# Transposing DMAs for half of x's first chunk, wq on a second queue and q in two passes, in a fused attention and GLU kernel

## The chip, the cores and the metric

The kernel runs on one core of one Trainium2 chip. The metric is device time in microseconds, the median of several executions. One execution is also profiled by the hardware; durations and waits come from that one.

## The reference

x is 2048 tokens of 512 features in bfloat16 (`A_x`; `B_x` is not read). Two branches work on the same x and are mixed by a gate per token:

```python
g = _sigmoid((x * gate_w).sum(-1, keepdims=True))
a = _A_ref(x, A_wq, A_wk, A_wv, A_wo, A_beta)
b = _B_ref(x, B_W_gate, B_W_up, B_W_down)
return g * a + (1 - g) * b
```

Branch A is attention with 32 heads of 16 features over four segments of 512 tokens: q, k and v are products of x with 512x512 weights; inside a segment the heads do causal softmax attention, and across segments a memory M and its normalizer z collect phi(k)·v and phi(k) of the earlier segments, which phi(q) reads. Both results are blended by a gate per head and multiplied by wo. Branch B is a gated linear unit: relu(x W_gate) * (x W_up), 1792 wide, times W_down.

## The kernel before

One program without loops on the chip. Python code lists every operation with its cost, its reads and its writes; a planner (`Sched`, lines 129 to 541) then walks through simulated time and decides, engine by engine, which ready operation comes next. It adds the semaphore waits, and so the order of the instructions on every engine is fixed when the kernel is built. The planner breaks ties by a pseudo-random number from `seeds` (line 567), one seed for each 8 us (`WIN`) of planned TensorE time; beyond the end of the tuple the last seed is used. `LAND0` (line 36) tells the planner how long after issue some of the first loads land, in ns; other loads get general figures. A DMA takes one of 16 semaphores.

Tokens are cut into four chunks of 512 that are also the segments. For each, the work is: the projections `proj` (L793 for q and k, with features on partitions; L791 for v, with tokens on partitions), the attention visits of `att` (L913 scores in row-tiled matmuls, L929 exp on ACT, L935 masks on POOL, L969 P·V, L979 and the following lines on DVE, ending in `oT`), the memory terms (L836, L856), the GLU (`ffn`, L1043 with L1051 to L1054), and `outp`, which sums W_down's product (L1082) and wo's product (L1075) in one PSUM bank, scales it (L1091, L1092) and stores it (L1094). A score visit takes four PSUM banks and is listed ahead of the rest of PE's work; the GLU's and projections' matmuls fill the time between visits.

The head, up to some 13 us, is what the change touches:

- Loads. SP issues two loads of x's first chunk, 256 KB each, tokens on partitions (`hT0` and `hT2`, which borrow the tile hT), then wq, wk, wv in four loads of 128 KB each, the first halves of W_gate and W_up, and more. ACT issues three 1 KB loads (`touch0` to `touch2`) and begins with an activation that loads its table (`tab`).
- `warm`: eleven matmuls on constants (L693) while the loads are on their way.
- Transposes of x's first chunk on TensorE: for each half h of 256 tokens and each kt of four blocks of 128 features two matmuls with an identity (L707) into a bank; DVE or ACT then copies the bank to xT (L714), which has features on partitions. The half h is a range of tokens, `xT0_{kt}` for h = 0 and `xT0_{kt + 4}` for h = 1. The later chunks of x come by transposing DMAs of 128 KB each (L621).
- q of the first segment: 16 matmuls of 512 tokens, kt outermost, the four columns of 128 features innermost. Each waits for wq's block kt and both halves of x's block kt. Then k, column by column, two kt to an operation, waiting for all of xT; then v.

Of the kernel before, what the change touches and what calls it, by code (L numbers as in the profile page):

```python
# [32 lines left out]
H1_T = 14000.0  # L33
LX = 300.0
DCOST = {"ldwg0_0": 1000.0, "ldbraw": 1800.0, "ldgwb": 1300.0, "ldx1_0": 1500.0, "vsh0": 1100.0, "vsh1": 1100.0, "vsh2": 1100.0, "vsh3": 1100.0}
LAND0 = {"ldhT0": 2850.0, "ldhT2": 3100.0, "ldwq0": 3150.0, "ldwq1": 3200.0, "ldwq2": 3100.0, "ldwq3": 3000.0}
NBLK = 36
QTN, EKN, HTN, OTN, XR = 8, 4, 19, 8, 3
SBX = 0
# [521 lines left out]
def build_kernel(nc, A_x, A_wq, A_wk, A_wv, A_wo, A_beta, W_g, W_u, W_d, gate_w, out):  # L561
    _, S, D = A_x.shape
    F = W_g.shape[1]
    assert D == 512 and S % 512 == 0 and F % 128 == 0
    NSEG, KT, NF, NT = S // 512, D // 128, F // 128, S // 128
    EPS, SCALE = 1e-6, 16 ** -0.5
    sc = Sched(seeds=(237719, 74891, 0, 89398, 0, 53401, 416309, 0, 0, 0, 710933, 0, 718714, 120896, 538430, 820480, 585027, 870794, 793690, 0, 589972, 0, 0, 0, 454998, 16783, 0,))
    T = {}
    with contextlib.ExitStack() as stack:
        for name, shape, dt in plan(S, D, F):  # L570
            T[name] = stack.enter_context(nc.sbuf_tensor(name, shape, dt))
        PS = stack.enter_context(nc.psum_tensor("ps", [128, 8, 512], F32))
        for st in sc.streams:
            sc.sem[st] = stack.enter_context(nc.semaphore(f"s_{st}"))
        program(sc, nc, T, PS, A_x, A_wq, A_wk, A_wv, A_wo, A_beta, W_g, W_u, W_d, gate_w, out, NSEG, KT, NF, NT, EPS, SCALE)
        with nc.Block() as block:
            sc.emit(block)
    return sc


def program(sc, nc, T, PS, A_x, A_wq, A_wk, A_wv, A_wo, A_beta, W_g, W_u, W_d, gate_w, out, NSEG, KT, NF, NT, EPS, SCALE):
# [19 lines left out]
    def act(fn, occ, **k):  # L601
        return op("act", fn, occ, **k)
# [15 lines left out]
    def load(eng, names, dst, src, nbytes, occ=474.0):  # L618
        (lact if eng == "act" else lsp).append(dma(eng, lambda e, dst=dst, src=src: e.dma_start(dst, src), nbytes, occ=occ, writes=names, name="ld" + names[0]))
# [5 lines left out]
        for kt in range(KT):  # L625
            load_xt("sp", c, kt)
    x0 = A_x[0, 0:512, :].rearrange("(h p i) d -> h p i d", h=2, i=2)
    for h in range(2):
        load("sp", [f"hT{2 * h}", f"hT{2 * h + 1}"], V.hT[:, 2 * h:2 * h + 2, :], x0[h], 1 << 18)
    for eng, nm, w, src in (("sp", "wq", V.wq, A_wq), ("sp", "wk", V.wk, A_wk), ("sp", "wv", V.wv, A_wv)):  # L630
        for kt in range(KT):
            load(eng, [f"{nm}{kt}"], w[:, kt, :], src[kt * 128:(kt + 1) * 128, :], 1 << 17)
    half = (NF // 2) * 128
# [9 lines left out]
    load("sp", ["gwb"], V.gwb[:, :], gate_w.partition_broadcast(128), 1 << 17)  # L643
    load("sp", ["braw"], V.braw[:], A_beta.partition_broadcast(128), 8192)
    load_gu(1)
    lact.insert(0, act(lambda e: e.activation(V.eb[:, 0:8], nc.const_aps.tensor(1.0, [128, 8], BF16), ACT.Exp), 1450, writes=["eb"], name="tab"))
    for n, w in enumerate((W_g, W_u, W_d)):
        load("act", [f"touch{n}"], V.adT[0:16, 32 * n:32 * n + 32], w[0:16, 0:32], 1024)
    sc.queue(0, lact)
    sc.queue(0, lsp)  # L650
    lsp = []
# [43 lines left out]
        return pe(fn, m * n * (0.834 if k == 0 else 0.5), writes=[f"bankL{b}"], name=f"warm{k}")  # L695

    xps, xcs = [warm(5, 512, 0, 3), warm(6, 128, 0, 3)], {"dve": [], "act": []}
    for h, kt, bank, eng in ((0, 0, 0, "dve"), (0, 1, 1, "act"), (0, 2, 2, "act"), (1, 0, None, "dve"), (0, 3, 3, "dve"), (1, 1, 0, "act"), (1, 2, 1, "dve"), (1, 3, 2, "act")):
        ep = Epoch("att") if bank is None else None
        bk = [] if bank is None else [f"bankL{bank}"]  # L700

        def B(ep=ep, bank=bank):
            return A(ep) if bank is None else PL[:, bank, :]

        def fx(e, h=h, kt=kt, B=B):
            for i in range(2):
                ins = e.matmul(B()[:, 128 * i:128 * i + 128], lhsT=V.hT[:, 2 * h + i, kt * 128:(kt + 1) * 128], rhs=V.ident[:], start=True, stop=True)  # L707
            return ins
        xps.append(pe(fx, 205, reads=[f"hT{2 * h}", "ident"], writes=bk, name=f"xt{4 * h + kt}", ep=ep, role=ep and "w"))
        dst = V.xT[:, kt, h * 256:(h + 1) * 256].rearrange("q (t i) -> q t i", i=2)  # L710

        def cpy(e, d=dst, B=B, eng=eng):
            x = B()[:, 0:256].rearrange("q (i t) -> q t i", i=2)
            return e.tensor_copy(d, x) if eng == "dve" else e.activation(d, x, ACT.Copy)  # L714
        xcs[eng].append(op(eng, cpy, 430 if eng == "dve" else 390, reads=bk, writes=[f"xT0_{kt + 4 * h}"], name=f"xc{4 * h + kt}", ep=ep, role=ep and "r"))
# [63 lines left out]
    def proj(s):  # L779
        pes, evs, sbs, acts, sps = [], [], [], [], []  # L780
        tok = s % XR * 512

        def pj(w, col, name, wname, tokmajor=False):
            early = s == 0 and name == "q"
            ep = Epoch("proj", 1, col) if s == 0 and name == "k" and col < 2 else Epoch("att" if early else "proj")
            step = 1 if early else 2
            for k0 in range(0, KT, step):
                def fn(e, k0=k0):
                    for kt in range(k0, k0 + step):
                        if tokmajor:  # L790
                            ins = e.matmul(A(ep)[:, :], lhsT=V.xT[:, kt, tok + col * 128:tok + (col + 1) * 128], rhs=w[:, kt, :], start=(kt == 0), stop=(kt == KT - 1))  # L791
                        else:
                            ins = e.matmul(A(ep)[:, :], lhsT=w[:, kt, col * 128:(col + 1) * 128], rhs=V.xT[:, kt, tok:tok + 512], start=(kt == 0), stop=(kt == KT - 1))  # L793
                    return ins
                pes.append(pe(fn, mm(512, step), reads=[f"{wname}{kt}" for kt in range(k0, k0 + step)] + ([f"xT0_{k0}", f"xT0_{k0 + 4}"] if early else xt(s)), name=f"{name}{s}_{col}", ep=ep, role="w2" if k0 else "w"))
            return ep
        def cp(fn, **k):
            return sc.add(Op([("dve", lambda e: fn(e, e.tensor_copy), t_dve(512)), ("act", lambda e: fn(e, lambda d, x: e.activation(d, x, ACT.Copy)), t_act(512))], **k))
        for G in range(4):
            ep = pj(V.wq, G, "q", "wq")  # L800
            qs = qslot(s, G)
            evs.append(cp(lambda e, f, ep=ep, qs=qs: f(V.qT[:, qs, :], A(ep)[:, :]), writes=[f"qT{qs}"], name=f"qcp{s}_{G}", ep=ep, role="r"))
            if s > 0 and G % 2:
                phi(s, "q", G, V.phiq, "phiq", V.qT, qs - 1, [f"qT{qs - 1}", f"qT{qs}"], acts, sbs)
            ep = pj(V.wk, G, "k", "wk")
            evs.append(cp(lambda e, f, ep=ep, G=G: f(V.kT[:, G, :], A(ep)[:, :]), writes=[f"kT{G}"], name=f"kcp{s}_{G}", ep=ep, role="r"))
            ks = kslot(s, G)
            kv = V.kT[:, G, :].rearrange("q (c k) -> q c k", c=8)
            for p in range(2):
                km = lambda e, kv=kv, p=p, ks=ks: e.tensor_scalar(V.kp[:, ks, :, 64 * p:64 * p + 64], kv, V.pm[:, p:p + 1], None, ALU.mult)  # L810
                ka = lambda e, kv=kv, p=p, ks=ks: e.activation(V.kp[:, ks, :, 64 * p:64 * p + 64], kv, ACT.Copy, scale=V.pm[:, p:p + 1])
                evs.append(sc.add(Op(([("dve", km, 380), ("act", ka, 715)] if s else [("dve", km, 380)]), reads=[f"kT{G}", "pm"], writes=[f"kp{ks}_{p}"], name=f"kmask{s}_{G}_{p}")))
            if s < NSEG - 1 and G % 2:
                phi(s, "k", G, V.ek, "ek", V.kT, G - 1, [f"kT{G - 1}", f"kT{G}"], acts, sbs)
                for g in (G - 1, G):
                    sps.append(dma("sp", lambda e, g=g: e.dma_start_transpose(V.phik[:, :, g * 128:(g + 1) * 128], V.ek[:, g % EKN, :]), 1 << 17, occ=1400.0, reads=[f"ek{g % EKN}"], writes=[f"phik{g}"], name=f"kT2{s}_{g}"))
        for tt in range(4):
            ep = pj(V.wv, tt, "v", "wv", True)
            evs.append(cp(lambda e, f, ep=ep, tt=tt: f(V.vaug[:, s % 2, tt, :, 0:16], A(ep)[:, :].rearrange("q (h c) -> q h c", c=16)), writes=[f"va{s % 2}_{tt}"], name=f"vcp{s}_{tt}", ep=ep, role="r"))
        if s == 0:  # L820
            qp = [[p for p in pes if p.name == f"q0_{col}"] for col in range(4)]
            pes = [qp[col][kt] for kt in range(4) for col in range(4)] + [p for k in "kv" for p in pes if p.name[0] == k]
        return pes, evs, sbs, acts, sps

    def va(s):
# [377 lines left out]
```

## Time and profile before

| | us |
|---|---|
| median of 3 executions | 264.2 (264.17 to 264.76) |
| the profiled execution | 264.5 |
| its span, first to last instruction | 262.7 |
| PE busy in the span | 255.7 |
| ACT busy | 184.5 |
| DVE busy | 179.1 |
| POOL busy | 131.0 |
| PE's first matmul on data (L707) | 3.69 |
| q's first matmul | 5.43 |
| k's first matmul | 9.48 |
| first score visit | 12.60 |

The span is a little shorter than the time of the execution that it belongs to, since the time holds what lies around the program too. A row of the timeline is: start in us, duration in us, engine, line, operation, tile written and tiles read, shapes, number of instructions merged into the row, and in brackets the idle time ahead of it with what ended it. PE is the matmuls, PEld the loads of the stationary operand, which overlap them; SPq and ACTq are the queues that issue DMAs. DMA traffic is heaviest at the start: the DMA engines' mean busy share is 0.69 in the first 8 us and 0.96 in the next 8.

### The profile page before, as it was taken

To read this page: it belongs to the slowest core of one execution; us is meant where nothing else is said; L and a number is where in the kernel's file an instruction comes from. 1 tells how busy PE (TensorE), PEld (TensorE's weight loads), DVE (VectorE), ACT (ScalarE), POOL (GpSimd) and SP (SyncE) were. 2 spreads that over 40 slices of the span, in tenths; PEclk is the share of its full clock that TensorE was granted. 3 is DMA by queue.
4 is the path that set the end of the run, shared out by engine and by line. 5 is a ranking of instruction groups with operands and counts; after the bars stand their busy time and mean duration, and the time that the engine had idled before them with its cause. 6 is when DMAs were issued, how large, how long until landed. Compare 5 with 4: busy or idle time off the path is not lost.

```text
span 262.7 us, 6432 instructions
## 1 busy us (share of the span) xinstructions
PE 255.7 (97%) x2619; PEld 114.6 (44%) x2653; DVE 179.1 (68%) x356; ACT 184.5 (70%) x160; POOL 131.0 (50%) x295
## 2 busy tenths in 40 slices
PE   8999999999999999999999999999999999999996
PEld 5444443444443544334444544443444444344444
DVE  5488878789986587778788676757667716477600
ACT  4586689999789779785768787677777665676021
POOL 3036557564646466666555457836365354545100
PEclk9999999999999999999999999999999999999999
DMA  6989646930261134213040242010131101000011
GB/s 197 286 302 281 138 66 148 274 44 22 68 155 25 24 81 117 48 22 33 10 107 13 59 91 23 4 40 2 31 76 40 22 24 34 26 2 2 0 42 40
DMA packets 34925, 19.87 MB, mean 76 GB/s; under 512 B 24016, under 2 KB 34128, under 8 KB 34896
## 3 DMA queue, kind: packets, MB, share of 16 engines
q1 hardware_dynamic: 34800, 19.46, 30.4%
q8 instruction: 21, 0.34, 0.6%
q14 instruction: 8, 0.07, 0.1%
q10 hardware_dynamic: 96, 0.00, 0.0%
HBM read 10.40 MB, written 2.11 MB: 48 GB/s over the span
## 4 chain that ended last, share of the span: by engine, by line
PE 97%; issue 1%; DVE 1%
PE ps L1043 38%; PE ps L1082 19%; PE ps L793 11%; PE ps L913 9%; PE ps L969 6%; PE ps L791 5%; PE ps L1075 5%; PE ps L856 1%; PE ps L693 1%; PE ps L707 1%; PE ps L836 0%; DVE hT L1054 0%; DVE Tn L979 0%; DVE osb L746 0%; DVE osb L1091 0%
## 5 line engine op out<-in xcount | busy, mean ns | idle before, releaser
L935 POOL TENSOR_SCALAR_AFFINE_SELECT E<-E 64x256 bf16<-64x256 bf16 (+1 forms) x256 | 111.1, 445 | 111.9 <-ACT E L929 82.7
L929 ACT ACTIVATE E<-ps 128x2048 bf16<-128x2048 f32 x72 | 135.1, 1876 | 38.7 <-PE ps L913 38.6
L1043 PE MATMUL ps<-xT,wu 128*128 128x512 bf16 x213 | 57.2, 380 | 1.4 <-issue 1.3
L1043 PE MATMUL ps<-xT,wg 128*128 128x512 bf16 x219 | 57.7, 380 | 0.6 <-issue 0.3
L1082 PE MATMUL ps<-wd,hT 128*128 128x512 bf16 (+2 forms) x229 | 52.8, 367 | 0.9 <-issue 0.6
L1054 DVE TENSOR_TENSOR hT<-ps,rl 128x512 bf16<-128x512 f32 x56 | 38.5, 687 | 16.5 <-PE ps L1043 16.4
L1082 PEld LDWEIGHTS ps<-wd,hT 128*128 128x128 bf16 x238 | 21.4, 98 | 23.8 <-issue 2.4
L1043 PEld LDWEIGHTS ps<-xT,wg 128*128 128x128 bf16 x224 | 20.6, 98 | 25.7 <-issue 2.8
L1043 PEld LDWEIGHTS ps<-xT,wu 128*128 128x128 bf16 x224 | 20.1, 98 | 25.4 <-issue 3.5
L913 PE MATMUL ps<-qT,kp 32*128 32x192 bf16 (+7 forms) x512 | 28.6, 287 | 0.0
L979 DVE STREAM_TRANSPOSE Tn<-ps 128x512 f32<-128x512 f32 x32 | 21.3, 696 | 9.1 <-PE ps L969 9.1
L1052 DVE TENSOR_SCALAR rl<-ps 128x512 bf16<-128x512 f32 x30 | 20.7, 690 | 8.2 <-PE ps L1043 7.9
L1091 DVE TENSOR_SCALAR osb<-ps,omg 128x512 bf16<-128x512 f32 (+1 forms) x8 | 5.6, 700 | 26.0 <-PE ps L1082 15.1
L1051 ACT ACTIVATE rl<-ps 128x512 bf16<-128x512 f32 x26 | 15.5, 598 | 9.9 <-PE ps L1043 9.7
L913 PEld LDWEIGHTS ps<-qT,kp 32*128 32x128 bf16 x512 | 8.2, 92 | 25.3 <-issue 13.1
L969 PE MATMUL ps<-E,vaug 64*17 64x128 bf16 (+7 forms) x512 | 18.7, 283 | 0.0
L969 PE MATMUL ps<-E,vsh 64*17 64x128 bf16 (+7 forms) x512 | 18.3, 283 | 0.0
L1092 ACT ACTIVATE osb<-ps,omg 128x512 bf16<-128x512 f32 (+1 forms) x9 | 6.1, 675 | 16.4 <-PE ps L1075 14.0
L793 PE MATMUL ps<-xT,wq 128*128 128x512 bf16 x61 | 16.1, 391 | 0.4 <-issue 0.3
L1075 PE MATMUL ps<-wo,oT 128*128 128x512 bf16 (+2 forms) x67 | 16.2, 366 | 0.2 <-issue 0.2
L793 PE MATMUL ps<-xT,wk 128*128 128x512 bf16 x60 | 15.6, 380 | 0.4 <-issue 0.3
L791 PE MATMUL ps<-wv,xT 128*128 128x512 bf16 x63 | 15.3, 380 | 0.1
(68 smaller groups left out, 229.2 us busy)
## 6 DMA issues: line engine op xcount, KB each, us to landing
vsh<-vaug SPq DMA_DIRECT2D x8, 272.0 KB, 4.3
osb<-in_A_x_dram SPq DMA_DIRECT2D x16, 128.0 KB, 2.3
out_dram<-osb SPq DMA_DIRECT2D x15, 128.0 KB, 1.7
wg<-in_B_W_gate_dram SPq DMA_DIRECT2D x8, 224.0 KB, 5.0
wu<-in_B_W_up_dram SPq DMA_DIRECT2D x8, 224.0 KB, 5.9
wd<-in_B_W_down_dram SPq DMA_DIRECT2D x1, 1792.0 KB, 10.5
hT<-in_A_x_dram SPq DMA_DIRECT2D x2, 256.0 KB, 3.0
wq<-in_A_wq_dram SPq DMA_DIRECT2D x4, 128.0 KB, 3.3
```

Of the source, the lines that this page charges most:

```text
L791: ins = e.matmul(A(ep)[:, :], lhsT=V.xT[:, kt, tok + col * 128:tok + (col + 1) * 128], rhs=w[:, kt, :], start=(kt == 0), stop=(kt == KT - 1))
L793: ins = e.matmul(A(ep)[:, :], lhsT=w[:, kt, col * 128:(col + 1) * 128], rhs=V.xT[:, kt, tok:tok + 512], start=(kt == 0), stop=(kt == KT - 1))
L913: ins = q.matmul(dst, lhsT=V.kp[r, kslot(s, G), c, :], rhs=V.qT[r, qslot(s, G), q0:q0 + w], start=True, stop=True, tile_position=(32 * jj, ...
L929: acts.append(act(lambda a: a.activation(V.E[:, base * 512:base * 512 + min(2048, 4 * W)], PF[:, 0:min(2048, 4 * W)], ACT.Exp, scale=SCALE ...
L935: pools.append(pool(lambda g, ap=ap, lim=lim, pat=pat: g.affine_select(out=ap, in_=ap, compare_op=ALU.is_ge, fill=0.0, base=lim, pattern=[ ...
L969: ins = q.matmul(A(eps[p])[32 * jj:32 * jj + 17, 64 * (c + u):64 * (c + u + n)], lhsT=v[:, 8 * G + 2 * jj + p, :], rhs=V.E[r, f:f + 64 * n ...
L979: ds.append(dve(lambda e, p=p, ep=eps[p]: e.transpose(V.Tn[:, 2 * (G % (TNN // 2)) + p, :], A(ep)[:, :]), t_dve(512), writes=[f"Tn{2 * (G ...
L1043: ins = e.matmul(A(ep)[:, :], lhsT=w[:, kt, f * 128:(f + 1) * 128], rhs=V.xT[:, kt, c % XR * 512:(c % XR + 1) * 512], start=(kt == 0), sto ...
L1052: ("dve", lambda e, ep=eg, r=r: e.tensor_scalar(V.rl[:, r, :], A(ep)[:, :], 0.0, None, ALU.max), t_dve(512))],
L1054: evs.append(dve(lambda e, ep=eu, r=r, hs=hs: e.tensor_tensor(V.hT[:, hs, :], A(ep)[:, :], V.rl[:, r, :], ALU.mult), t_dve(512), reads=[f" ...
L1075: ins = e.matmul(A(ep)[:, 0:c1 - c0], lhsT=V.oT[:, ot[G], i * 128:(i + 1) * 128], rhs=V.wo[:, G, c0:c1], start=st_ and G == 0, stop=sp_ an ...
L1082: ins = e.matmul(A(ep)[:, 0:c1 - c0], lhsT=V.hT[:, slots[f], i * 128:(i + 1) * 128], rhs=V.wd[:, f, c0:c1], start=st_ and f == f0, stop=sp ...
```

## The change

The second half of x's first chunk (tokens 256 to 511) no longer comes through hT, TensorE and a copy. Four transposing DMAs on SP, one for each block of 128 features, 64 KB each, write it to xT directly; they stand behind `hT0`'s load and ahead of wk's. Four of the eight transposing operations on PE (eight matmuls) and four copies go; the remaining four copies are all DVE's. wq's four loads go to ACT's queue, behind `touch0`, and `tab` goes behind all of ACT's loads. q's products are made in two passes of 256 tokens, first all kt and columns for the first half of the tokens, then for the second, 32 matmuls for 16; each waits for its own half alone. The first two columns of k are issued kt by kt, the two columns side by side. The planner's landing times for the first loads are restated, and its tuple of seeds is a new one of 33 numbers for 27, so the order of instructions after the head is another one too.

```diff
-LAND0 = {"ldhT0": 2850.0, "ldhT2": 3100.0, "ldwq0": 3150.0, "ldwq1": 3200.0, "ldwq2": 3100.0, "ldwq3": 3000.0}
+LAND0 = {"ldhT0": 2950.0, "ldxb0": 3900.0, "ldxb1": 3950.0, "ldxb2": 4000.0, "ldxb3": 4050.0, "ldwq0": 2900.0, "ldwq1": 3150.0, "ldwq2": 3400.0, "ldwq3": 3700.0, "ldwk0": 3900.0, "ldwk1": 3900.0, "ldwk2": 3900.0, "ldwk3": 3950.0}
...
-    for h in range(2):
-        load("sp", [f"hT{2 * h}", f"hT{2 * h + 1}"], V.hT[:, 2 * h:2 * h + 2, :], x0[h], 1 << 18)
-    for eng, nm, w, src in (("sp", "wq", V.wq, A_wq), ("sp", "wk", V.wk, A_wk), ("sp", "wv", V.wv, A_wv)):
+    load("sp", ["hT0", "hT1"], V.hT[:, 0:2, :], x0[0], 1 << 18)
+    for kt in range(KT):
+        lsp.append(dma("sp", lambda e, kt=kt: e.dma_start_transpose(V.xT[:, kt, 256:512], A_x[0, 256:512, kt * 128:(kt + 1) * 128]), 1 << 16, occ=660.0, writes=[f"xT0_{kt + 4}"], name=f"ldxb{kt}"))
+    for eng, nm, w, src in (("act", "wq", V.wq, A_wq), ("sp", "wk", V.wk, A_wk), ("sp", "wv", V.wv, A_wv)):
...
-    lact.insert(0, act(lambda e: e.activation(V.eb[:, 0:8], nc.const_aps.tensor(1.0, [128, 8], BF16), ACT.Exp), 1450, writes=["eb"], name="tab"))
+    tab = (act(lambda e: e.activation(V.eb[:, 0:8], nc.const_aps.tensor(1.0, [128, 8], BF16), ACT.Exp), 1450, writes=["eb"], name="tab"))
     for n, w in enumerate((W_g, W_u, W_d)):
         load("act", [f"touch{n}"], V.adT[0:16, 32 * n:32 * n + 32], w[0:16, 0:32], 1024)
+    lact = lact[4:5] + lact[:4] + lact[5:] + [tab]
...
-    for h, kt, bank, eng in ((0, 0, 0, "dve"), (0, 1, 1, "act"), (0, 2, 2, "act"), (1, 0, None, "dve"), (0, 3, 3, "dve"), (1, 1, 0, "act"), (1, 2, 1, "dve"), (1, 3, 2, "act")):
+    for h, kt, bank, eng in ((0, 0, 0, "dve"), (0, 1, 1, "dve"), (0, 2, 2, "dve"), (0, 3, 3, "dve")):
...
-            step = 1 if early else 2
+            first = s == 0 and name == "k" and col < 2
+            step = 1 if early or first else 2
...
+                if early:
+                    for h in range(2):
+                        def fh(e, k0=k0, h=h):
+                            return e.matmul(A(ep)[:, 256 * h:256 * h + 256], lhsT=w[:, k0, col * 128:(col + 1) * 128], rhs=V.xT[:, k0, 256 * h:256 * h + 256], start=(k0 == 0), stop=(k0 == KT - 1))
+                        pes.append(pe(fh, mm(256), reads=[f"{wname}{k0}", f"xT0_{k0 + 4 * h}"], name=f"{name}{s}_{col}", ep=ep, role="w2" if k0 + h else "w"))
+                    continue
...
-            pes = [qp[col][kt] for kt in range(4) for col in range(4)] + [p for k in "kv" for p in pes if p.name[0] == k]
+            kp = [[p for p in pes if p.name == f"k0_{col}"] for col in range(2)]
+            pes = [qp[col][2 * kt + h] for h in range(2) for kt in range(4) for col in range(4)] + [kp[col][kt] for kt in range(4) for col in range(2)] + [p for k in "kv" for p in pes if p.name[0] == k and p.name not in ("k0_0", "k0_1")]
```

More of the change, by code (lines that the diff above doesn't have):

```diff
@@ L566, in build_kernel @@
     EPS, SCALE = 1e-6, 16 ** -0.5
-    sc = Sched(seeds=(237719, 74891, 0, 89398, 0, 53401, 416309, 0, 0, 0, 710933, 0, 718714, 120896, 538430, 820480, 585027, 870794, 793690, 0, 589972, 0, 0, 0, 454998, 16783, 0,))
+    sc = Sched(seeds=(140892, 423927, 526636, 0, 0, 29334, 773274, 197051, 969207, 716731, 932006, 619180, 627323, 133294, 0, 462444, 160517, 80860, 908900, 0, 153406, 228141, 875880, 487918, 463495, 96319, 0, 0, 0, 804673, 0, 975897, 0,))
     T = {}
@@ L794, in fn @@
                     return ins
-                pes.append(pe(fn, mm(512, step), reads=[f"{wname}{kt}" for kt in range(k0, k0 + step)] + ([f"xT0_{k0}", f"xT0_{k0 + 4}"] if early else xt(s)), name=f"{name}{s}_{col}", ep=ep, role="w2" if k0 else "w"))
+                if early:
[4 more added lines that the diff above has]
+                    continue
+                pes.append(pe(fn, mm(512, step), reads=[f"{wname}{kt}" for kt in range(k0, k0 + step)] + xt(s), name=f"{name}{s}_{col}", ep=ep, role="w2" if k0 else "w"))
             return ep
```

## The prediction

> **What bounds the kernel now.** I read the page's first parts, then the engine waits of PE, then the timeline of the first 14 us.
>
> ```profile
> span 262.7 us, 6432 instructions
> PE 255.7 (97%) x2619; PEld 114.6 (44%) x2653; DVE 179.1 (68%) x356; ACT 184.5 (70%) x160; POOL 131.0 (50%) x295
> ...
> PE 97%; issue 1%; DVE 1%
> ```
>
> PE is busy for 97% and the chain that ended last is PE for 97%. The 7.0 us without PE are 0.84 at the start, 2.2 after the last matmul (260.46, by the timeline of the end) and 4.0 between. The waits of PE tell what the 4.0 are (us in total, times, longest):
>
> ```profile
> PE ps L1043 <- issue: 1.6, 10, 0.2
> PE ps L693 <- PEq L1188: 0.8, 1, 0.8
> ...
> PE ps L1043 <- DVE Tn L979: 0.2, 1, 0.2
> ```
>
> Only one entry, of 0.2 us, is a wait for data of another engine; the rest are gaps of about 0.16 us when PE comes back from a row-tiled visit (the scores of L913, the P·V of L969). So the time follows PE's own work and the number of its visits. The stage that the change touches is the head; its PE and PEld rows (start, us, engine, line, tiles, count):
>
> ```profile
> 0.84 2.93 PE L693 MATMUL ps<-const-bfloat16-1.0 128*128 128x512 bf16 x11 [0.84 <-PEq L1188]
> 3.69 1.95 PE L707 MATMUL ps<-ident,hT 128*128 128x128 bf16 x16
> ...
> 5.43 4.21 PE L793 MATMUL ps<-xT,wq 128*128 128x512 bf16 x16
> ...
> 5.86 0.15 PEld L793 LDWEIGHTS ps<-xT,wq 128*128 128x128 bf16 x1 [0.28 <-issue]
> 6.29 0.15 PEld L793 LDWEIGHTS ps<-xT,wq 128*128 128x128 bf16 x1 [0.28 <-issue]
> 6.68 2.47 PEld L793 LDWEIGHTS ps<-xT,wq 128*128 128x128 bf16 x12 [0.24 <-issue]
> ```
>
> PE runs without a break from 0.84 on. Its weight loads stand 0.43 us apart up to 6.29 and then twelve stand in 2.47 (0.21 each): until about 6.7 us a 512-column matmul takes 0.43, afterwards 0.216. The granted clock reads 1.00 in every stretch, so only this spacing shows the slow start. In the chain of waits the head has no hole either:
>
> ```profile
> 3.77 1.87 PE ps L707 x16
> 5.64 5.30 PE ps L793 x22
> ...
> 256.53 2.28 PE ps L1082 x14
> ...
> 259.46 0.78 PE ps L1082 x14
> ```
>
> A PE transpose costs 1.87 / 16 = 0.117 us there. The last two lines are 14 matmuls of 384 and of 128 columns at the full clock: 0.163 and 0.056 each, new weights for every one.
>
> **The change, part by part.**
>
> *Eight PE transposes go* (h = 1: four tiles, two matmuls each). At 0.117 that is 0.94 us of slow-clock time. If the clock still rises at 6.7, what moves into that time would otherwise run at the double rate: 0.47. Followed through: transposes 3.77 to 4.71; the first copy is ready at 4.12 + 0.42 = 4.54, so q starts at 4.71. In the 2.0 us to 6.7 it does 2.0 / 0.215 = 9.3 half matmuls.
>
> *q in halves.* 32 matmuls of 256 columns for 16 of 512. No row has this form at the full clock; between the 0.056 of 128 columns and the 0.163 of 384 lies 0.109, and half of 0.216 is 0.108: sixteen more instructions cost 0.02 us at that, and (0.163 - 0.109) x 22.7 = 1.2 us if the weight load (98 ns busy in its row) could no longer hide and a half took as long as 384 columns. I take 0.109, as the 128-column row shows weights hidden under a still shorter matmul. The other 22.7 halves take 2.47, and q ends at 9.17. Before: 5.64 + 2.5 x 0.43 + 13.5 x 0.216 = 9.63. **Head: -0.46.**
>
> Rule and row: the Trainium skill, "TensorE: Matmul & The Clock Gate", section "Part 1: The HAM clock gate (the "warmup" mystery)", holds that the clock rises after some 3.4 us of sustained activity, in a window of time that runs free, and not after a number of matmuls. By that the removed work counts at the full-clock price, about half; if the rise moved with the work done, the gain would be the whole 0.94 (a rival below).
>
> *wq on ACT's queue.* ACT issues touch0 at 0.87 and then one load every 0.45: 1.30, 1.77, 2.2, 2.65. wq landed 3.1 to 3.6 us after issue, so the four land at 4.4-4.9, 4.9-5.4, 5.3-5.8, 5.8-6.3. They are needed at 4.71, 5.56, 6.41 and 7.0. At worst wq0 is 0.2 late in slow-clock time: 0 to +0.1; I take 0. Behind them on ACT stand touch1, touch2 and the table load with its activation (1.28 + 0.21), now at about 4.0 to 5.5; ACT's next work is the copy of q at about 8.7, so 3 us cover it. Four ACT copies (0.38 each) leave.
>
> *Four transposing DMAs on SP.* They take the place of one load of x and four of wq: SP reaches wk at 0.81 + 0.45 + 4 t, against 3.62. No 64 KB transpose is in the trace; the 128 KB ones bound it:
>
> ```profile
> L621 SPq DMA_TRANSPOSE xT<-in_A_x_dram x12: 1122/1260/3257, 17.6 to 70.6; - x12
> ...
> DMA to landing us min/median/max: 2.5/3.7/9.2
> ```
>
> With t between 0.47 (a plain issue) and 1.26, wk starts between 3.15 and 6.3; half the bytes speak for 0.66 (3.9, +0.28). The transposes issue at 1.26, 1.92, 2.58, 3.24; at the median landing of 3.7 they are there at 5.0 to 6.9. Pass two needs them at 7.4, 7.9, 8.3, 8.7: cover of 1.8 for the last. Landing at 2.5 gains nothing, at 6.0 (the one issued at 17.6 behind full queues) the last is 0.5 late: 0 to +0.5; I take 0, since only hT0, three transposes and wq, 0.96 MB, are ahead of it and the DMA row of 4 to 8 us moves 264 GB/s. wk lands 3.4 after its issue, 7.3 against 9.17 needed; wv moves by 0.28 too and has 3 us; the last wu of the first half, issued at 10.7 and landing 5.5 later, would come at 16.5 and is needed near 18. Nothing else is on SP's queue until gwb.
>
> *k's columns 0 and 1 kt by kt.* The same eight matmuls, with finer waits; column 0 is finished 0.4 us later after q, column 1 as before, and PE has k2, k3 and v to run until the first visit (12.6). Zero. *The four copies on DVE alone* end near 5.8, needed at 7.0. Zero.
>
> *The order anew.* The same instructions. Going through PE's timeline visit by visit, fifteen of the sixteen P·V runs already stand beside a score visit; each further joined or parted visit is worth 0.16 (the gap) + 0.11 (a visit takes 0.33 for 0.21 of streaming) = 0.27. Downward that is three or four visits, -0.9; upward three and a new data wait, about +1.5. Since neither side is nearer I take 0.
>
> **Sum:** -0.46 against the profiled execution: span 262.7 to 262.2, its time 264.5 (1.8 around the span) to 264.0. That execution stood 0.3 above the median of 264.2, so the median should be **263.75, say 263.8**. A difference under 0.3% (0.8 us) can't be told from no change here.
>
> **Rivals.**
> *Better order* (0.22): three visits joined. The lone P·V run near 244.5 and five lone runs of L856 leave room; the empty list of data waits speaks against more. -0.46 - 0.8: 262.9.
> *The clock rises with the work* (0.14): -0.94, 263.3. One execution can't tell time from work; the rise would have to move with the eight transposes.
> *The tail loses its cover* (0.13), the one on the other side. The last P·V ends near 245.6 and its DVE chain gives oT at 249.64:
>
> ```profile
> 245.79 5.13 PE L1082 MATMUL ps<-wd,hT 128*128 128x512 bf16 x23 [0.16 <-issue]
> ...
> 249.21 0.43 DVE L998 TENSOR_TENSOR oT<-oTt,amemT 128x512 bf16<-128x512 bf16 x1
> ...
> 250.75 1.89 PE L1075 MATMUL ps<-wo,oT 128*128 128x512 bf16 x8
> ```
>
> 23 matmuls cover it with 1.0 us to spare. A new order that keeps 11 for this place leaves 2.6 us less, a hole of 1.6 us: 264.2 - 0.46 + 1.6 = 265.3. It makes the kernel slower by 0.3% from a hole of 1.25, fewer than 13 matmuls. For it: the whole order after the head is new. Against it: the end lists L1082 ahead of L1075 by construction.
> *The transposes don't come in time* (0.16). At t = 1.26 the last is issued at 5.0; landing 3.7 later it comes at the point of need, and wk, from 6.3 on, lands 9.7 and costs 0.5: 264.2, the gain eaten, the change not doing what it says (0.08). At a landing of 6.0 it comes at 11.0, 2.3 late: 266.0 (0.08). It decides from a landing after 9.2, and makes the kernel slower by 0.3% from 10.0.
>
> The Trainium skill, "DMA: Bandwidth & Descriptors", section "Issuing engines are not separate DMA queues", speaks against the move of wq: a second issuing queue saves only issue time, since all share the same 16 DMA engines. The trace's shares of 0.84 in 4 to 8 us and 0.98 in 8 to 12 us leave little room for more; by that rule the 0.4 us by which wq is issued earlier would not all reach the landing, which ends in the rival just above.
>
> **How the numbers follow.** Forecast 0.35 (own range 263.4 to 264.4). Faster by over 0.3%: better order and the work clock, 0.36. Within: the forecast and the eaten gain, 0.43. Slower: tail 0.13 and late transposes 0.08, 0.21. To leave out no more than 2 in 10 the range reaches from below the better order, 262.4, to the tail's hole, 265.4.
>
> **What would show it.** Right: eight L707 matmuls, q's first matmul near 4.7 and its last ending near 9.2 without a wait, SP issues of about 0.66 us, wk from 3.9, PE's waits still nearly all "issue", 14 or more matmuls between the last P·V and L1075. Wrong: a DMA wait on PE at L793 or its successor line, a clock spacing that turns before 6 us, data waits among PE's, or a sum of gaps that differs from 4.0 by over a microsecond.

## The result and the profile after

The changed kernel takes 267.61 us (median of 6 executions, 266.82 to 268.32) against 264.2 of the kernel before: a ratio of 1.0125, 95% interval 1.0103 to 1.0147. It is slower by 3.4 us, outside the range that was forecast and on the other side. The profiled execution took 267.03 with a span of 265.3, 2.6 longer than the span before.

The page's first parts of the changed kernel:

```profile
span 265.3 us, 6477 instructions
PE 258.9 (98%) x2661; PEld 114.4 (43%) x2661; DVE 177.5 (67%) x351; ACT 186.2 (70%) x161; POOL 128.5 (48%) x295
...
PE 92%; SPq 4%; DMA 2%; issue 0%; DVE 0%
```

PE is still the chain for nearly the whole span, but 6% of it are now SP's queue and a DMA. The waits of PE (us in total, times, longest) say where:

```profile
PE ps L1053 <- DMA wg<-in_B_W_gate_dram: 2.4, 1, 2.4
PE ps L695 <- PEq L1198: 0.8, 1, 0.8
PE ps L801 <- DMA wq<-in_A_wq_dram: 0.4, 1, 0.4
PE ps L801 <- DVE xT L716: 0.2, 1, 0.2
```

One wait of 2.4 us for W_gate stands out; before there was no wait for a DMA among PE's matmuls. The timeline of the head (start, us, engine, line, tiles, count) shows how it comes about; first the changed kernel, then four rows of the kernel before:

```profile
1.25 1.95 ACTq L619 DMA_DIRECT2D wq<-in_A_wq_dram  x4
1.26 5.04 SPq L630 DMA_TRANSPOSE xT<-in_A_x_dram  x4
...
6.35 2.00 SPq L619 DMA_DIRECT2D wk<-in_A_wk_dram  x4
...
9.02 3.71 PE L796 MATMUL ps<-xT,wk 128*128 128x512 bf16 x16
...
10.30 1.85 SPq L619 DMA_DIRECT2D wg<-in_B_W_gate_dram  x4
...
12.57 0.59 PE L794 MATMUL ps<-wv,xT 128*128 128x512 bf16 x2
...
15.58 0.60 PE L1053 MATMUL ps<-xT,wg 128*128 128x512 bf16 x2 [2.42 <-DMA wg<-in_B_W_gate_dram]
```

```profile
3.62 1.86 SPq L619 DMA_DIRECT2D wk<-in_A_wk_dram  x4
...
7.42 1.85 SPq L619 DMA_DIRECT2D wg<-in_B_W_gate_dram  x4
...
9.48 3.19 PE L793 MATMUL ps<-xT,wk 128*128 128x512 bf16 x13
...
17.26 1.03 PE L1043 MATMUL ps<-xT,wg 128*128 128x512 bf16 x4
```

Four transposing DMAs hold SP from 1.26 to 6.30. wk is issued at 6.35, 2.7 us later than before (3.62), and W_gate at 10.30, 2.9 later (7.42). Up to k nothing is lost: k starts at 9.02, 0.46 ahead of the 9.48 before, the forecast gain, though it came about in another way (see "The head's gain" below). But the new order has PE do two matmuls of v at 12.57 and then two that need W_gate's first two blocks, which land at 15.0 and 15.5. v's other matmuls, whose data is there, stand behind them. The group of line L630 (min/median/max ns of one issue, then the times to landing):

```profile
L630 SPq DMA_TRANSPOSE xT<-in_A_x_dram x4: 1188/1237/1244, 1.3 to 5.1; - x4
...
DMA to landing us min/median/max: 2.9/3.7/4.6
```

A 64 KB transposing DMA holds the queue for 1.24 us, about as long as one of 128 KB (1.26 in the trace of before).

### The profile page after: what moved, and what is told of

It is laid out like the page before. It is cut to its first block, busy times and chain, and to the rows that moved or that the text cites. A ratio compares the mean times of both kernels' runs of the same rounds, so it can differ in the third digit from the quotient of the medians.

```text
span 265.3 us, 6477 instructions
## 1 busy us (share of the span) xinstructions
PE 258.9 (98%) x2661; PEld 114.4 (43%) x2661; DVE 177.5 (67%) x351; ACT 186.2 (70%) x161; POOL 128.5 (48%) x295
## 3 DMA queue, kind: packets, MB, share of 16 engines
HBM read 10.14 MB, written 2.11 MB: 46 GB/s over the span
## 4 chain that ended last, share of the span: by engine, by line
PE 92%; SPq 4%; DMA 2%; issue 0%; DVE 0%
PE ps L1053 38%; PE ps L1092 19%; PE ps L923 9%; PE ps L796 8%; PE ps L979 7%; PE ps L1085 5%; PE ps L794 5%; SPq L619 2%; DMA wu<-in_B_W_up_dram 2%; SPq L630 2%; PE ps L866 1%; PE ps L846 1%; DVE osb L1101 0%
## 5 line engine op out<-in xcount | busy, mean ns | idle before, releaser
L945 POOL TENSOR_SCALAR_AFFINE_SELECT E<-E 64x256 bf16<-64x256 bf16 (+1 forms) x256 | 108.7, 435 | 112.3 <-ACT E L939 83.0
L1053 PE MATMUL ps<-xT,wg 128*128 128x512 bf16 x224 | 59.8, 380 | 2.4 <-DMA wg<-in_B_W_gate_dram 2.4
L1053 PE MATMUL ps<-xT,wu 128*128 128x512 bf16 x224 | 59.8, 380 | 0.1
L1092 PE MATMUL ps<-wd,hT 128*128 128x512 bf16 (+2 forms) x238 | 54.8, 367 | 0.0
L1061 ACT ACTIVATE rl<-ps 128x512 bf16<-128x512 f32 x26 | 15.5, 596 | 7.0 <-PE ps L1053 6.5
L1102 ACT ACTIVATE osb<-ps,omg 128x512 bf16<-128x512 f32 (+1 forms) x12 | 8.1, 678 | 16.6 <-PE ps L1085 14.0
L796 PE MATMUL ps<-xT,wk 128*128 128x512 bf16 x64 | 16.4, 380 | 0.0
L979 PEld LDWEIGHTS ps<-E,vaug 64*17 64x17 bf16 x512 | 11.6, 86 | 8.7 <-issue 4.4
L1002 POOL TENSOR_TENSOR adT<-Tn,rdg 128x512 bf16<-128x512 f32 x12 | 12.6, 1054 | 2.3 <-DVE rdg L1000 2.3
```

The source lines that it names most:

```text
L945: pools.append(pool(lambda g, ap=ap, lim=lim, pat=pat: g.affine_select(out=ap, in_=ap, compare_op=ALU.is_ge, fill=0.0, base=lim, pattern=[ ...
L979: ins = q.matmul(A(eps[p])[32 * jj:32 * jj + 17, 64 * (c + u):64 * (c + u + n)], lhsT=v[:, 8 * G + 2 * jj + p, :], rhs=V.E[r, f:f + 64 * n ...
L1053: ins = e.matmul(A(ep)[:, :], lhsT=w[:, kt, f * 128:(f + 1) * 128], rhs=V.xT[:, kt, c % XR * 512:(c % XR + 1) * 512], start=(kt == 0), sto ...
L1092: ins = e.matmul(A(ep)[:, 0:c1 - c0], lhsT=V.hT[:, slots[f], i * 128:(i + 1) * 128], rhs=V.wd[:, f, c0:c1], start=st_ and f == f0, stop=sp ...
```

## The experiments

Two theories stood at the outset. "Issue": the fixed price of issuing a transposing DMA makes every later load on SP late, and PE waits. "Transposition": the transposing itself burdens the DMA engines. A third, "order", puts the loss on the new order alone. The planner lays out a new order whenever a figure changes, and that alone moves the time; so most of these kernels keep the order of PE, DVE and POOL of the changed kernel to the instruction and exchange only DMAs behind the same semaphores. Ratios are to the kernel before on the same chip, with 95% intervals.

**plain64.**

```diff
-        lsp.append(dma("sp", lambda e, kt=kt: e.dma_start_transpose(V.xT[:, kt, 256:512], A_x[0, 256:512, kt * 128:(kt + 1) * 128]), ...
+        lsp.append(dma("sp", lambda e, kt=kt: e.dma_start(V.xT[:, kt, 256:512], A_x[0, 128 * kt:128 * kt + 128, 256:512]), ...
```

> The changed kernel with every engine's order kept; the four transposing DMAs become four plain loads of the same 64 KB each into the same places. The transposition of tokens 256 to 511 is left out. Theory 'issue' (a transposing DMA holds SP for 1.24 us whatever its size, so W_gate and W_up come 2.5 us later than the order was laid out for, and PE waits): SP reaches wk at about 3.2 instead of 6.35, PE's wait of 2.4 us for W_gate and the 0.6 for W_up are gone, 264.3 +- 0.5. Theory 'transposition' (the crossbar work itself slows the DMA engines): also about 264.3. Theory 'order' (the new order is bad in itself): 266.5 or more.

264.64 us, ratio 1.0025 [1.0008, 1.0041]. The timeline of its head:

```profile
1.26 1.83 SPq L630 DMA_DIRECT2D xT<-in_A_x_dram  x4
3.13 1.85 SPq L619 DMA_DIRECT2D wk<-in_A_wk_dram  x4
...
6.93 1.85 SPq L619 DMA_DIRECT2D wg<-in_B_W_gate_dram  x4
```

W_gate is issued 3.4 us earlier, and the same pair of its matmuls starts at 12.99, without a wait. The order as such therefore costs little: the new order with timely loads, and with no transposing in the head, is some 0.7 us (0.2 to 1.1) above the kernel before. Since both kernels run the same visits in the same order, their starts can be subtracted: the first score visit is at 14.39 instead of 16.98 (2.6), the tenth at 41.61 instead of 44.51 (2.9); from the fifteenth on the difference stays at 2.4, as plain64 meets a wait of its own near 57 us (0.8 on the weight load of L796, for DVE's Tn). The loss of the change lies wholly in the first 20 us.

**plain64_slow.**

```diff
-        lsp.append(dma("sp", lambda e, kt=kt: e.dma_start_transpose(V.xT[:, kt, 256:512], ...
+        lsp.append(dma("sp", lambda e, kt=kt: [e.dma_start(V.xT[:, kt, 256:512], A_x[0, 128 * kt:128 * kt + 128, 256:512])] + [e.dma_start(V.oTt[0:16, 64 * kt + 32 * j:64 * kt + 32 * j + 32], A_x[0, 0:16, 0:32]) for j in range(2)], ...
```

> As plain64, but each 64 KB load is followed by two loads of 1 KB, so that SP is held for about 1.3 us per block as by a transposing DMA, with no transposition anywhere in the head. The transposition of tokens 256 to 511 is left out. Theory 'issue': SP reaches wk at about 6.3 again, PE waits for W_gate for about 2.4 us, 267.2 +- 0.6. Theory 'transposition': no such wait, 264.5. Theory 'order': 266.5 or more, like plain64.

267.74 us, 1.0148 [1.0133, 1.0163]: the changed kernel's time again, without a single transposition in the head. The waits of PE:

```profile
PE ps L1053 <- DMA wg<-in_B_W_gate_dram: 1.2, 1, 1.2
...
PE ps L1053 <- DMA wu<-in_B_W_up_dram: 0.8, 1, 0.8
PE ps L796 <- DMA wk<-in_A_wk_dram: 0.8, 2, 0.4
PE ps L801 <- DVE xT L716: 0.5, 1, 0.5
```

wk goes at 6.86 here. The waits for loads are spread over wk, W_gate and W_up (2.8 in all) rather than gathered on W_gate. With plain64 this shows that lateness on SP's queue can by itself cost as much as the change does. It is no exact copy: SP is held 0.5 us longer than in the changed kernel, and yet W_gate's first pair starts earlier (14.89 against 15.58). What part of the 2.4 us of wait goes back to W_gate's longer landing in the changed kernel (4.7 us for its first block, 3.6 here) is not shown.

**one256_same.**

```diff
     for kt in range(KT):
-        ... e.dma_start_transpose(V.xT[:, kt, 256:512], A_x[0, 256:512, kt * 128:(kt + 1) * 128]) ...
+        ... (lambda e: e.dma_start_transpose(V.xT[:, :, 256:512], A_x[0, 256:512, :])) if kt == 0 else (lambda e, kt=kt: e.dma_start(V.oTt[0:16, 32 * kt:32 * kt + 32], A_x[0, 0:16, 0:32])) ...
```

> The changed kernel with every engine's order kept; the four transposing DMAs of 64 KB become one of 256 KB and three plain loads of 1 KB. Nothing of the computation is left out. If the issue of a transposing DMA has a fixed price, SP is held 1.26 + 3 x 0.45 = 2.6 us, wk goes at about 3.9, no wait for W_gate: theory 'issue' 264.4 +- 0.6. If its price follows the bytes beyond 128 KB, about 2.5 + 1.35 and wk at 5.1, a wait of about 1.2: 265.6. Theory 'transposition': the same bytes are transposed, so the wait stays near 2.4 and the time near 267.

265.4 us, 1.0068 [1.0043, 1.0094]. The group of L630 and, below it, PE's waits:

```profile
L630 SPq DMA_TRANSPOSE xT<-in_A_x_dram x1: 1317/1317/1317, 1.3 to 1.3; - x1
```

```profile
PE ps L801 <- DMA wq<-in_A_wq_dram: 1.3, 1, 1.3
```

256 KB are issued in 1.32 us: the price is per DMA and hardly depends on the bytes. The wait for W_gate is gone, as "issue" says. But the time is 0.4 above the expected span, and another wait is there: wq's second block landed 4.8 us after its issue, against 3.8 in plain64, whose plain loads of x were issued at the same time, and 3.2 in the changed kernel. The transposing DMA was issued 0.5 us before that block and landed at 6.78, the block at 6.57. wq's last block landed at 7.58 instead of 6.87 in plain64, and k starts at 10.20 instead of 9.33. So "transposition" is not nothing; it has its own, smaller price.

**xb_act_same.**

```diff
     sc.run()
+    sp, ac = sc.prog["sp"], sc.prog["act"]
+    ...
+    for i, j in zip(ia, ib):
+        ac[i], sp[j] = sp[j], ac[i]
```

> The changed kernel with the order of PE, DVE, POOL kept and two groups of DMAs exchanged: the four transposing DMAs are issued by ACT, wq's four loads by SP. Nothing of the computation is left out. Theory 'issue' (1.24 us of the issuing queue per transposing DMA is what costs, and on ACT nothing is queued behind them but two 1 KB loads and the table load): SP reaches wk at about 3.1, no wait for W_gate or W_up, 264.6 +- 0.5, as with plain loads. Theory 'transposition': 267, as the changed kernel.

265.79 us, 1.0056 [1.0038, 1.0075], 0.7 above the expected span: better than the changed kernel by more than half of the loss, yet not as good as plain loads. PE's waits:

```profile
PE ps L801 <- DMA xT<-in_A_x_dram: 1.1, 2, 0.7
...
PE ps L801 <- DMA wq<-in_A_wq_dram: 0.5, 1, 0.5
```

SP reaches wk at 3.22 and no weight of the GLU is late. In exchange SP's plain loads are now issued while ACT issues its transposes one every 1.27 us, and these land 4.6 to 5.1 us after issue (2.9 to 4.6 in the changed kernel, with SP's plain loads held up behind them). The last block comes at about 10.1, and q's second pass waits for it.

**xb2_act_same and act256_late** exchange the DMAs in the same way, with fewer transposes (the part that exchanges the queues is left out):

```diff
+        ... e.dma_start_transpose(V.xT[:, 2 * kt:2 * kt + 2, 256:512], A_x[0, 256:512, kt * 256:(kt + 1) * 256]) if kt < 2 else e.dma_start(V.oTt[0:16, 32 * kt:32 * kt + 32], A_x[0, 0:16, 0:32]) ...
```

```diff
+        ... e.dma_start_transpose(V.xT[:, :, 256:512], A_x[0, 256:512, :]) if kt == 0 else e.dma_start(V.oTt[0:16, 32 * kt:32 * kt + 32], A_x[0, 0:16, 0:32]) ...
```

> As xb_act_same (order of PE, DVE and POOL as in the changed kernel, transposes on ACT's queue, wq on SP's), but with two transposing DMAs of 128 KB and two plain loads of 1 KB in place of four of 64 KB. Nothing of the computation is left out. If the price of a transposing DMA is fixed, the last one is issued at 2.5 instead of 5.1 and q's waits of 0.4 and 0.7 us for it go away; SP stays free and W_gate early: 264.6 +- 0.5, level with the plain loads. If the landing follows the transposed bytes rather than the issue, the waits stay and the time is 265.5 or more.

264.78 us, 1.0020 [1.0010, 1.0030], as expected; the profiled execution took 265.36. Two DMAs of 128 KB take 1.27 each, and the waits for x are gone, as the fixed price says. The waits of PE for loads in the head are for wq, 1.3 us in three pieces:

```profile
PE ps L801 <- DMA wq<-in_A_wq_dram: 1.3, 3, 0.6
```

> As xb2_act_same, with a single transposing DMA of 256 KB, issued by ACT at about 2.2 behind two loads of 1 KB, so that wq's first blocks are ahead of it. Nothing of the computation is left out. Theory: wq lands as with plain loads (wait under 0.3), x's second half lands 4.5 to 5.5 after issue, 6.7 to 7.7, when q's second pass begins: 264.6 +- 0.5. Rival (a transposing DMA holds back the loads around it wherever it stands): wq or x is waited for by 1 us or more, 265.5 or more.

265.67 us, 1.0076 [1.0046, 1.0105]: the rival. With the single DMA behind two small ones PE still waits 1.4 us for wq (1.0 at the longest). A part of that wait comes of PE being ready sooner in this execution (see "The clock" below); the landings tell it more safely. wq's last three blocks land 0.3 to 0.8 us later than in plain64, the last at 7.64 instead of 6.87, and k starts 0.8 later (10.14). So a transposing DMA of 256 KB held back wq's loads when issued at 1.3 and when issued at 2.2.

**told_ss** (the planner told the true price, new seeds searched for it):

```diff
-... occ=660.0, writes=[f"xT0_{kt + 4}"], name=f"ldxb{kt}"))
+... occ=1240.0, writes=[f"xT0_{kt + 4}"], name=f"ldxb{kt}"))
-LAND0 = {"ldhT0": 2950.0, "ldxb0": 3900.0, ...
+LAND0 = {'ldhT0': 2700.0, 'ldxb0': 3400.0, ..., 'ldwg0_0': 4700.0, ..., 'ldwu0_3': 5500.0}
```

> The changed kernel, with the planner told 1.24 us for the issue of a transposing DMA and landing times of the first loads as measured, and seeds searched anew for that. All of the change's instructions are there; the order is another. Theory 'issue' in its wider form (the loads come late in any case, but the wait arises only because the order put W_gate's product ahead of v's): wk still goes at 6.35, v stands ahead of the GLU, PE's wait for W_gate under 0.5, about 265.3. Rival (with W_gate 4 us late PE has nothing to do in its place): the wait is over 1.5 and the time 266.5 or more.

266.39 us, 1.0074 [1.0047, 1.0101]. v now stands ahead of the GLU and the wait for W_gate is gone, but W_up is waited for twice:

```profile
PE ps L1053 <- DMA wu<-in_B_W_up_dram: 1.0, 2, 0.6
```

The order takes off a part of the loss, not all of it: once v is done at 16.7, the GLU is the only work left beside the visits, and its loads come late in this order too. The time is above the expectation by 1.1, of which these two waits are 1.0.

**two128_s** (two DMAs of 128 KB on SP, seeds searched):

```diff
+    for j in range(2):
+        lsp.append(dma("sp", lambda e, j=j: e.dma_start_transpose(V.xT[:, 2 * j:2 * j + 2, 256:512], A_x[0, 256:512, j * 256:(j + 1) * 256]), 1 << 17, occ=1280.0, ...
```

> Two transposing DMAs of 128 KB (tokens 256 to 511, two blocks of features each) for four of 64 KB, the planner told so, seeds searched. If the price of issue is fixed per DMA, SP reaches wk at 3.85 and no load is late; what is left is the gain of the head (0.46) and the order found: 264.7 +- 0.7. If the price follows the bytes or the blocks, wk goes at 6.3 and the time is 266 or more.

266.18 us, 1.0092 [1.0057, 1.0127], a miss by 0.8 beyond the expected span. wk goes at 3.90, as the fixed price says, and no load of SP is late; wq is waited for three times, 1.1 us in all, v runs before the first visit, which comes only at 17.12, and the order that was found has 84 runs of row-tiled and memory work between PE's other matmuls, where the kernel before has 77. What such a run costs was not measured, and how the remainder divides between these was not taken apart.

**seeds_only and head_only** exchange the two tuples of seeds:

```diff
-    sc = Sched(seeds=(237719, 74891, 0, ...
+    sc = Sched(seeds=(140892, 423927, 526636, ...
```

> The kernel before with the changed kernel's 33 seeds and nothing else of the change: its head, another order after it. Theory 'issue': the order matters by the number of visits only, 264.2 +- 0.8. Theory 'order': a new order costs of itself, 266 or more.

267.47 us, 1.0132 [1.0117, 1.0147]: "issue" missed here. With the head before and no late SP queue, seeds that belong to another head cost as much as the change itself: 82 such runs for 77, and waits of 0.7 for W_gate (again GLU matmuls put ahead of v), 0.8 for oT at 87.8 us, 0.9 in smaller ones (E, wq, hT).

> The changed kernel with the seeds of the kernel before: all of the change but the new seeds. Theory 'issue': W_gate comes at 15 us as in the changed kernel; an order not searched for this head costs on top of it what the new seeds cost the old head (some 3 us): 268 to 271. Theory 'order' alone: 265 to 267.

269.31 us, 1.0186 [1.0145, 1.0227]: the time is in the span that "issue" gave, but not by the waits that it named. This order has v ahead of the GLU, so PE does not wait for W_gate at all, though SP's loads are as late as in the changed kernel (W_gate issued at 10.31); W_up costs 0.5. The longest wait is elsewhere, near 37.7 us, for the transposed copy of ek that the memory terms read:

```profile
PE ps L846 <- DMA phik<-ek: 1.6, 1, 1.6
```

So the late loads cost 2.4 us at W_gate only with an order that puts its product ahead of v. What the two runs show is that seeds cost time with a head that they were not searched for: 3.4 us with the head before, and 1.7 us on top of the changed kernel with the changed head.

## Why the prediction was wrong

*The step that failed* is the term of SP's queue: "half the bytes speak for 0.66 (3.9, +0.28)". A 64 KB transposing DMA holds the queue 1.24 us, and 128 KB and 256 KB hold it 1.27 and 1.32. The price was bounded from both sides, 0.47 and 1.26, and the value in between was taken on the assumption that it follows the bytes, which no row of the trace bore: all its transposes had the same size. The three sizes put the value at the upper end. SP's queue was late by 2.7 us instead of 0.28 (wk at 6.35, at the forecast's upper bound of 6.3).

*The rival was half right.* "The transposes don't come in time" named t = 1.26, but priced only x's last block and wk (0.5) and came to 264.2, or to 266.0 with late landings of x, which did not happen (2.9 to 4.6 us). wk cost little, since it landed 2.2 to 2.4 us after issue instead of 3.4. Of what stood behind wk on the same queue, W_gate was followed nowhere, W_up's last block in the forecast at t = 0.66 alone, and neither in the rival. In the changed kernel they make 2.4 us of wait and the 0.6 by which the weight load of W_up's first pair is late.

*The order anew* was taken as 0, with bounds of -0.9 and +1.5. Two things were wrong in it. The cover of each load was read from the order before, in which the GLU begins at 17.3 behind all of v; the new order wants W_gate at 13.2. And the bound upward was too narrow: seeds_only shows +3.4. In the changed kernel itself the order costs little beyond that: plain64, same order and timely loads, is 0.25% above the kernel before.

*The head's gain* came out as forecast, in part by luck. The working took the clock to rise at 6.7 and wq to cost no wait. In the profiled execution of the changed kernel the clock rose at about 3.9, so PE was ready earlier and then waited 0.4 for wq, whose last block landed at 6.78 instead of 6.3 at the latest; that block, not the clock, set the end of q. told_ss has the same head, and there the clock rose at about 6.7. Its q runs without a wait, and k starts at 9.09, 0.39 earlier than before, which is the forecast's own way. The rows of the changed kernel, then of told_ss:

```profile
3.57 0.73 PE L709 MATMUL ps<-ident,hT 128*128 128x128 bf16 x8
```

```profile
3.57 1.06 PE L709 MATMUL ps<-ident,hT 128*128 128x128 bf16 x8
...
4.51 4.75 PE L801 MATMUL ps<-xT,wq 128*128 128x256 bf16 x32
...
9.09 3.72 PE L796 MATMUL ps<-xT,wk 128*128 128x512 bf16 x16
```

A half matmul took 0.11 at the full clock, as taken. In plain64 the gain is 0.15, as wq's second block comes 0.2 late and part of q still runs at the slow clock.

*wq on ACT's queue*: its first block lands at 3.9 instead of 5.1, its last at about 6.8 as before (3.1 + 3.6 = 6.7). The Trainium skill's rule in "DMA: Bandwidth & Descriptors", section "Issuing engines are not separate DMA queues", that a second queue saves issue time alone, agrees for the last of the four blocks, which gained nothing; the first, ahead of which a load of 256 KB no longer stands, came 1.2 us earlier. That this would end in late transposes was the wrong conclusion: in the changed kernel PE waits 0.4 for wq, and its matmuls never for x's second half.

*The transposition* was given no price on the DMA engines. In the first 8 us plain64 moved 231 GB/s at a busy share of 0.77, one256_same 190 at 0.87, xb2_act_same 172 at 0.85. If plain bytes cost 0.77 x 8 / (231 x 8 / 1000) = 3.3 us of all engines per MB, the 0.26 MB transposed took 2.8 and 3.1, some three times as much per byte: an estimate from these three rows. By this estimate the rule in "Advanced Engine Details and Errata", section "X-Bar Transpose (TRN2)", of the Trainium skill, that transposing DMAs are as fast as regular ones, does not hold here for x's rows of 512 and 1024 bytes; the measurement decides.

*The clock* was taken to rise at 6.7 in the changed kernel too. By the starts of single instructions on PE, whose spacing halves at the rise, it rose at about 6.5 in the kernel before, 3.9 in the changed kernel, 6.7 in told_ss, and between some 3.6 and 6 in the other nine profiled executions. The changed kernel and told_ss have the same matmuls in the same order up to there; 13 of them came before the rise in the one, 29 in the other. So it does not follow the work done, and the rival that ties it to that found no support; nor does it come at a fixed time. PE's busy time in the first 12 us differs by 0.8 between these two executions (10.39 and 11.16), more than the 0.46 that the head was to gain, so a difference of that size between two single profiles need not come from the kernels.

*The tail* kept its cover: among PE's waits in the changed kernel there is none for oT.

None of the ten kernels is faster than the kernel before. The best one that computes all of it, xb2_act_same, is 0.2% slower.

## What to carry to other kernels

A DMA has a price on the queue that issues it besides its bytes: count it for every instruction, and follow everything behind it on that queue to the first consumer in the *new* order, not only the next load. A transposing DMA is better issued in fewer pieces and from a queue with nothing urgent behind it; the largest piece was not the best here: on ACT's queue two of 128 KB cost 0.2%, four of 64 KB 0.6% and one of 256 KB, issued later, 0.8%. And when a hand-made or searched order goes with a change, keep that order fixed and exchange single parts under it: otherwise each experiment also measures a new order, which here is worth as much as the change.

## What was not expected

Holes of 0.16 us that the profile of the kernel before shows on PE are not waits. plain64 and the changed kernel have the same matmuls in the same order, but the page of plain64 counts 2628 and that of the changed kernel 2661. The same four matmuls of v after a visit, first in plain64, then in the changed kernel:

```profile
56.23 0.81 PE L794 MATMUL ps<-wv,xT 128*128 128x512 bf16 x3 [0.16 <-issue]
```

```profile
58.90 1.04 PE L794 MATMUL ps<-wv,xT 128*128 128x512 bf16 x4
```

In the first the record of one matmul is missing and leaves a hole ended by "issue"; in the second all four are there and so is no hole. From 20 to 240 us the changed kernel's PE is busy for all of the 220. The kernel before has 34 matmul records fewer than weight loads (2619 and 2653); the changed kernel has 2661 of each. So the prediction's reading of 4.0 us of gaps as the price of coming back from a visit, and the 0.16 in its figure of 0.27 for a visit more or less, came by all signs from missing records. Compare the count of an instruction with what the program must issue before a short idle piece is given a cause.
